# Linear attention with a routed feed-forward layer: accumulators of seven slots, token selection on ScalarE, and a bound order on GpSimd

## The chip, the cores and the metric

The kernel runs on one core of a Trainium2 chip. Its engines work beside one another, each through its own instructions in order: TensorE (PE in the profile; its weight loads are shown as PEld), VectorE (DVE), ScalarE (ACT), GpSimd (POOL) and SyncE (SP), which here only issues DMAs. The metric is the device time of one execution in microseconds (us), as the median of several runs.

## What is computed

A linear attention over 8 batches, 8 heads, 576 positions and head size 64, and behind it a layer of 8 experts in which each of the 4608 tokens goes to the one expert with the largest logit.

```python
def phi(x):
    proj = np.einsum('bhsd,df->bhsf', x, w_phi)                 # 64 -> 128
    proj = proj - np.max(np.abs(proj), axis=-1, keepdims=True)
    return np.concatenate([np.exp(proj), np.exp(-proj)], axis=-1)
q_p, k_p = phi(q), phi(k)
kv = np.einsum('bhsf,bhsd->bhfd', k_p, v)
z = np.sum(k_p, axis=2)
num = np.einsum('bhsf,bhfd->bhsd', q_p, kv)
den = np.einsum('bhsf,bhf->bhs', q_p, z)[..., None] + 1e-06
x = (num / den)                                                 # as rows: 4608 x 512
...
logits = x @ w_gate
expert_idx = np.argmax(logits, axis=1)
probs = softmax(logits)
h = np.maximum(xe @ w1[e], 0.0)                                 # xe: the rows of expert e
out[mask] = gate_w[mask, None] * (h @ w2[e])
```

## The kernel before

**Units and chunks.** The attention is worked in 16 units: four groups of two batches each (`NG`), and in each group four pairs of heads (`NPR`). The tokens of a group, 2 x 576, are nine chunks of 128 rows: chunks 0 to 3 are of the first batch, 4 to 7 of the second, and chunk 8, the tail, holds the last 64 rows of both. A unit goes through these stages:

- `load` and `split` bring k and q of the unit in two parts (three in unit 0) and write each as a rounded high part xh (on ACT) and a rest xl (mostly on POOL), since PE's products are made of three products of high and low parts.
- `project` multiplies by w_phi on PE (ps_proj) and subtracts the largest magnitude on DVE (tile t). `k_features` takes the two exponentials on ACT (tile e), `k_parts` splits them into kh (ACT) and kl: on POOL for chunk pairs 4 and 6, and from unit 1 on for pair 0, else on DVE. `q_features` transposes t on PE (pt) and takes the exponentials on ACT (qp).
- `v_parts` loads v and splits it into vh (ACT) and vl (POOL).
- `kv_steps` sums k's features against v on PE (pk, 30 products for each batch), `kv_copy` copies the sum on ACT (kvT), `fold_steps` multiplies it on PE with the tile fold (pf), which holds an identity and the gate's weights, so that one product later yields the numerator (64 columns), the denominator (1) and the gate's logits (8): 73 columns, `W`. DVE copies the result to kf.
- `num_steps` multiplies qp with kf on PE, into accumulators pn of six slots of 73 columns, with two buffers; a slot is a chunk of one of the two heads. There are four accumulators a unit: chunks 0 to 2, 3 to 5, 6 and 7, and the tail. Behind the last product of each, `normalize` or `normalize_tail` adds 1e-6 to the denominators, takes the reciprocal, and multiplies numerators (into xrow) and logits (into lgc), on DVE. After the tail, `store_rows` writes the unit's 128 columns of x to DRAM.

**What is done when.** Each unit has two halves. In the first, PE makes the sums over k and v of the previous unit's second batch, its fold, and the numerators of its chunks 0 to 3; in the second, the sums of its own first batch, and the previous unit's second fold and chunks 4 to 8. `half` writes the order of these products by hand and `ordered` binds it; the projections of the unit at hand and the next one are woven in by `merge`. What else runs when is set by a planner at build time: it goes through the program with assumed durations, gives each engine the earliest instruction in program order that is ready then, and so writes one fixed order for each engine, which the chip then follows with waits on semaphores. It moves work that is ready early far ahead: `constants2`, written in unit 2, runs at 13 us. `behind(m, other)` binds m behind other in the planner's order and adds no wait.

**Routing.** When a group's four units are done, `route` finds each token's expert, its rank in the expert and its gate: logits (a sum over lgc), largest logit, one-hot rows, counts, ranks, and then `select` for each of the nine chunks: two one-hot matrices of 128 x 128, with row number + 1 (sel_p) and the chunk's base (sel_h) in place of the one, from which PE later makes the list of tokens in each block. For groups 0 to 2 (`final is None`) the steps are spread over the units of the next group, one after every six products of a half (`spread`): the ranks and selections 0 to 6 fall into the second half of its second unit, selections 7 and 8 and the gate into the first half of its third. sel_p is made on DVE and sel_h on POOL. For the last group, routed in two parts, chunks 0, 2, 4, 6 and 8 are selected on ACT by `select_a`: y = |rank - column|, then relu(part1 - part1 * y), which is part1 where y is 0 and 0 elsewhere.

**Feed-forward.** After the attention, from 420 us on, blocks of 128 tokens are gathered by an indirect DMA, multiplied with the weights of their expert (split into wh on ACT and wl on DVE or POOL) and scattered to the output. `first_items` with the string `ORDER` writes the order of unit 0; there `C` stands for `constants`, which fills fold: a memset and eight copies on POOL, and a DMA of the gate's weights in ACT's queue.

Lines that come up: xl is L244, kl L284, kh L282, vl L312, kvT L353, pf L362, pn L386 (chunks) and L395 (tail), normalization L423 to L432 (tail L443 to L453), sel_p and sel_h L788, the ACT selection L780 to L782.

Of the kernel before, what the change touches and what calls it, by code (L numbers as in the profile page):

```python
# [9 lines left out]
F32 = mybir.dt.float32  # L10
# [3 lines left out]
AF = mybir.ActivationFunctionType  # L14
ALU = mybir.AluOpType
AX = mybir.AxisListType
# [3 lines left out]
P = 128  # L20
B, H, S, D = 8, 8, 576, 64
F = 128
DM = H * D
E = 8
# [3 lines left out]
NPR = H // 2  # L28
NC = 9
# [6 lines left out]
NU_ALWAYS = NU - 2  # L36

NSLOT = 7
NEARLY = (NG - 1) * NC
KD = DM // P  # L40
KF = FF // P
W = 73
# [7 lines left out]
def tile_linear_attention_moe(  # L50
# [12 lines left out]
    V, A, G, T = nc.vector, nc.scalar, nc.gpsimd, nc.tensor  # L63
# [21 lines left out]
    sm = late.enter_context(tc.tile_pool(name="sm", bufs=2, side="right"))  # L85
    sg = late.enter_context(tc.tile_pool(name="sg", bufs=1, side="right"))
    ps_kv = late.enter_context(tc.tile_pool(name="ps_kv", bufs=2, space=PSUM, side="right"))
    hold = mid.enter_context(tc.tile_pool(name="hold", bufs=1, side="right"))
    ps_nm = mid.enter_context(tc.tile_pool(name="ps_nm", bufs=2, space=PSUM, side="right"))
# [21 lines left out]
    fold = const.tile([D + 1, H, W], F32, name="fold")  # L111
# [8 lines left out]
    iota_p = const.tile([P, P], F32, name="iota_p")  # L120
# [4 lines left out]
    part1 = const.tile([P, 1], F32, name="part1")  # L125
    hb_i = const.tile([P, NG, NC], I32, name="hb_i")
    hbase = const.tile([P, NTILE], F32, name="hbase")
    neg1 = const.tile([P, 1], F32, name="neg1")
    neg_h = const.tile([P, NTILE], F32, name="neg_h")

    def constants():

        G.memset(fold, 0.0)
        for h in range(H):
            G.tensor_copy(fold[:, h, 0 : D + 1], ident[0 : D + 1, 0 : D + 1])
        nc.scalar.dma_start(fold[0:D, :, D + 1 : W], w_gate.rearrange("(h d) e -> d h e", d=D))
# [28 lines left out]
    sel_p = rt.tile([P, NTILE, P], BF16, name="sel_p")  # L165
    sel_h = rt.tile([P, NTILE, P], BF16, name="sel_h")
# [70 lines left out]
    def split(st, x, part, eh, el):  # L237

        n = st["ranges"][part][1] - st["ranges"][part][0]
        xr = st["raw", x, part]  # L240
        xh = inp.tile([P, CUT], F32R, name="xh", bufs=3)
        xl = inp.tile([P, CUT], F32R, name="xl", bufs=3)
        (A.copy if eh is A else eh.tensor_copy)(xh[:, 0:n], xr[:, 0:n])  # L243
        el.tensor_tensor(xl[:, 0:n], xr[:, 0:n], xh[:, 0:n], op=ALU.subtract)  # L244
        st["parts", x, part] = (xh, xl)

    def project(st, x, c0, n):
# [30 lines left out]
    def k_parts(st, c0, n):  # L278
        e, m = st["e", c0], 2 * n
        kh = kvp.tile([P, m, 2, F], F32R, name="kh", tag=f"kh{n}", bufs=3 * n - 1)  # L280
        kl = kvp.tile([P, m, 2, F], F32R, name="kl", tag=f"kl{n}", bufs=3 * n - 1)
        A.copy(kh, e[:, 0:m])  # L282
        eng = G if c0 in (4, 6) or (c0 == 0 and st["u"] > 0) else V
        eng.tensor_tensor(kl, e[:, 0:m], kh, op=ALU.subtract)  # L284
        for i in range(n):
            st["kp", c0 + i] = (kh, kl, 2 * i)

# [19 lines left out]
    def v_parts(st, u):  # L307
        vt = kvp.tile([P, NC * 2 + 2, D], F32, name="vt", bufs=1)
        nc.sync.dma_start(vt, vv[u])
        vh, vl = v_tiles[u % 2]  # L310
        A.copy(vh[:, :, 0:D], vt)
        G.tensor_tensor(vl, vt, vh[:, :, 0:D], op=ALU.subtract)  # L312
        st["v"] = (vh, vl)

    def v_load0(st, c0, c1):
# [62 lines left out]
    def num_steps(st, chunks):  # L378


        def step(c, hh, s):
            if c in (0, 3, 6, 8) and hh == 0 and s == 0:
                st["pn"] = ps_nm.tile([P, 6, W], F32, name="pn")
            qp, s0 = st["qp", c]
            if c < 8:
                m = T.matmul(  # L386
                    st["pn"][:, 2 * (c % 3) + hh, :],
                    qp[:, s, s0 + hh, :],
                    st["kf"][:, c // 4, hh, s, :],
                    start=(s == 0),  # L390
                    stop=(s == 1),
                )
            else:

                m = T.matmul(  # L395
                    st["pn"][:, 2 * hh : 2 * hh + 2, :],
                    qp[:, s, hh].rearrange("p b q -> p (b q)"),
                    st["kf"][:, :, hh, s, :],
                    start=(s == 0),
                    stop=(s == 1),  # L400
                )
            if c in (2, 5, 7, 8) and hh == 1 and s == 1:
                if c < 8:
                    normalize(st, c - c % 3, c % 3 + 1, st["pr"])
                else:
                    normalize_tail(st, st["pr"])
                    eng = G if st["g"] == NG - 1 and st["pr"] == 2 else nc.sync
                    store_rows(st["g"], st["x"], st["pr"] * P, P, eng=eng)
            return m

        return [
            (186 if c < 8 else 260, lambda a=(c, hh, s): step(*a))
            for c in chunks
            for hh in range(2)
            for s in range(2)
        ]

    def normalize(st, c0, n, pr):
        pn = st["pn"][:, 0 : 2 * n]
        if c0 == 0:  # L420
            st["x"] = hold.tile([P, NC, P], F32, name="xrow", bufs=2)
        rec = sm.tile([P, 6], F32, name="rec", bufs=2)[:, 0 : 2 * n]
        V.tensor_scalar_add(rec, pn[:, :, D], 1e-6)  # L423
        V.reciprocal(rec, rec)
        rb = rec.rearrange("p (c h) -> p c h", h=2).unsqueeze(3)
        V.tensor_tensor(
            st["x"][:, c0 : c0 + n, :].rearrange("p c (h d) -> p c h d", h=2),
            pn[:, :, 0:D].rearrange("p (c h) d -> p c h d", h=2),
            rb.to_broadcast([P, n, 2, D]),
            op=ALU.mult,  # L430
        )
        V.tensor_tensor(  # L432
            st["lgc"][:, c0 : c0 + n, 2 * pr : 2 * pr + 2, :],
            pn[:, :, D + 1 : W].rearrange("p (c h) e -> p c h e", h=2),
            rb.to_broadcast([P, n, 2, E]),
            op=ALU.mult,
        )

    def normalize_tail(st, pr):

        pn = st["pn"][:, 0:4].rearrange("p (h b) w -> p h b w", b=2)
        rec = sm.tile([P, 6], F32, name="rec", bufs=2)[:, 0:4].rearrange("p (h b) -> p h b", b=2)
        V.tensor_scalar_add(rec, pn[:, :, :, D], 1e-6)  # L443
        V.reciprocal(rec, rec)
        for b in range(2):
            rows = slice(D * b, D * b + D)
            V.tensor_tensor(
                st["x"][rows, 8, :].rearrange("p (h d) -> p h d", h=2),
                pn[rows, :, b, 0:D],
                rec[rows, :, b].unsqueeze(2).to_broadcast([D, 2, D]),  # L450
                op=ALU.mult,
            )
            V.tensor_tensor(  # L453
                st["lgc"][rows, 8, 2 * pr : 2 * pr + 2, :],
                pn[rows, :, b, D + 1 : W],
                rec[rows, :, b].unsqueeze(2).to_broadcast([D, 2, E]),
                op=ALU.mult,
            )

    def zipped(a, b):  # L460

# [13 lines left out]
    def behind(m, other):  # L475

        tc.add_manual_dep(
            m.ins,
            other.ins.name,
            mybir.DependencyInfo(mybir.DependencyClass.NoSync, mybir.DependencyReason.DATA),  # L480
            reason="order of the engine",
        )
# [164 lines left out]
    def route(g, lgc, c0, n, final=None):  # L647

        j0 = g * NC + c0
        js = slice(j0, j0 + n)  # L650
        r = {}
# [9 lines left out]
        def logits():  # L661
            V.tensor_reduce(
                tile_of("lg", [P, NC, E]),
                lgc[:, c0 : c0 + n].rearrange("p c h e -> p c e h"),
                axis=AX.X,
                op=ALU.add,
            )

# [115 lines left out]
        def select(c):  # L784
            if final is not None and c0 + c in ON_ACT:
                return select_a(c)
            for eng, dst, by in ((V, sel_p, part1), (G, sel_h, hbase[:, j0 + c : j0 + c + 1])):
                eng.tensor_scalar(  # L788
                    dst[:, j0 + c, :], iota_pb, r["rkr"][:, c : c + 1], by, op0=ALU.is_equal, op1=ALU.mult
                )  # L790
# [120 lines left out]
    for i in range(2):  # L911
        vh = kvp.tile([P, NC * 2 + 2, D + 2], F32R, name=f"vh{i}")
# [2 lines left out]
    deferred, prev = [], None  # L915
    units = []
    for g in range(NG):
        lgc = sm.tile([P, NC, H, E], F32, name="lgc")
        units += [{"u": g * NPR + pr, "g": g, "pr": pr, "lgc": lgc} for pr in range(NPR)]
    feats = feature_items(units[0], 0)  # L920
    for u, st in enumerate(units):
# [100 lines left out]
    st = {}  # L1022
# [19 lines left out]
    def weights(u, k):  # L1042
# [5 lines left out]
        w = max(0, u - 1)  # L1048
        slot = f"{k}_{w % 2}" if k < KD else f"s{(w * (NPC - KD) + k - KD) % NSLOT}"
        pool = wp0 if slot == "s0" or (k < KD and w % 2 == 0) else wp1 if slot in ("s1", "s2", "s3") else wpr  # L1050
# [153 lines left out]
    op = ctx.enter_context(tc.tile_pool(name="op", bufs=2, side="left", reuse_waits="tile"))  # L1204
# [151 lines left out]
```

## Time and profile before

| what | value |
|---|---|
| median of 3 runs | 924.06 us (922.11 to 924.46) |
| profiled execution | 923.96 us, span 922.3 us |
| mean granted clock of PE | 0.983 |
| PE busy, 50 to 75 us (a stretch of attention) | 24.81 of 25 us, clock 1.00 |
| PE busy, 0 to 25 us | 18.18 of 25 us, clock 0.93 |
| PE busy, 600 to 700 us (feed-forward) | 100.00 of 100 us, clock 1.00 |
| DVE, ACT, POOL busy over the span | 596.7, 590.5, 485.0 us |
| sel_p on DVE | 31 instructions, 18.8 us |
| normalization, multiplications of numerators | 32 of 128x384 at 551 ns, 16 of 128x256 at 421 ns, 32 of 64x128 at 286 ns |

How such lines are read: a group's row gives line, engine, operation, output and inputs with their shapes, the count, then busy time in us, the mean of one in ns, and the idle time of the engine just before them with what ended it. A timeline's row gives start and duration in us, engine, line, operation and tiles, how many were merged, and in brackets the idle time before it and what released it. A window's row gives its length, the busy time of PE, PEld, DVE, ACT and POOL with their instruction counts, PE's granted clock, the DMA share and GB/s. Idle time of an engine that nothing waits for costs nothing.

### The profile page before, as it was taken

Reading aid. Unit: us, or ns where it says so; the run is one execution under the profiler, and the core shown is the slowest. Engines: PE = TensorE matmul, PEld = TensorE weight load, DVE = VectorE, ACT = ScalarE, POOL = GpSimd, SP = SyncE. Lnnn points to the kernel's source line nnn. Section 1 sums busy time; section 2 is a strip of 40 time slices with the busy share of each in tenths; the row PEclk is TensorE's granted clock in tenths of the full one; section 3 lists DMA queues with packets and bytes.
Section 4 is the critical chain, followed back from the end, with each engine's and each line's share of the span. In section 5 each row is a group of like instructions: output and inputs, shape, how many; then the busy total and the mean of one; then the engine's idle time right before and its main releaser. Section 6 shows DMA issues by size and latency. Waiting matters only on the chain. (4 is left out here: it accounts for less than half of the span.)

```text
span 922.3 us, 18298 instructions
## 1 busy us (share of the span) xinstructions
PE 889.5 (96%) x6703; PEld 831.0 (90%) x6703; DVE 596.7 (65%) x1134; ACT 590.5 (64%) x900; POOL 485.0 (53%) x332
## 2 busy tenths in 40 slices
PE   7799999999999999999999999999999999999995
PEld 6799999999999999999799999999999999987883
DVE  7477788777987788759774444444444444457850
ACT  7577787777868776755565555555555555568951
POOL 7556668866676669734443333333333333337641
PEclk9799999999999999999999999999999999999998
DMA  5233433233334333243143143431434634764100
GB/s 154 80 96 107 107 106 103 68 100 102 93 93 108 106 107 93 76 129 108 59 154 122 45 152 115 155 112 44 153 114 158 215 113 149 229 206 129 46 24 15
DMA packets 64620, 102.44 MB, mean 111 GB/s; under 512 B 10702, under 2 KB 28622, under 8 KB 64528
## 3 DMA queue, kind: packets, MB, share of 16 engines
q1 hardware_dynamic: 57136, 80.31, 28.5%
q0 software_dynamic: 6720, 20.80, 7.3%
q8 instruction: 53, 0.87, 0.4%
q14 instruction: 39, 0.32, 0.1%
q10 hardware_dynamic: 672, 0.15, 0.1%
HBM read 136.81 MB, written 20.26 MB: 170 GB/s over the span
## 5 line engine op out<-in xcount | busy, mean ns | idle before, releaser
L1054 DVE TENSOR_TENSOR wl<-raw,wh 128x1024 fp32r<-128x1024 f32 x138 | 184.6, 1350 | 136.2 <-ACT wh L1053 136.1
L1053 ACT CAST wh<-raw 128x1024 fp32r<-128x1024 f32 x184 | 191.4, 1050 | 93.7 <-PE po L1120 66.2
L1054 POOL TENSOR_TENSOR wl<-raw,wh 128x1024 fp32r<-128x1024 f32 x46 | 113.3, 2469 | 175.0 <-ACT wh L1053 167.6
L386 PE MATMUL pn<-kf,qp 128*128 128x73 f32 x1024 | 156.8, 252 | 0.0
L1099 PE MATMUL pm<-xl,wh 128*128 128x256 f32 x544 | 154.1, 283 | 0.0
L1100 PE MATMUL pm<-xh,wl 128*128 128x256 f32 x544 | 154.1, 283 | 0.0
L1098 PE MATMUL pm<-xh,wh 128*128 128x256 f32 x544 | 153.4, 283 | 0.0
L386 PEld LDWEIGHTS pn<-kf,qp 128*128 128x128 f32 x1024 | 151.3, 190 | 0.1
L284 POOL TENSOR_TENSOR kl<-e,kh 128x1024 fp32r<-128x1024 f32 x47 | 112.4, 2392 | 50.7 <-ACT kh L282 47.9
L261 DVE TENSOR_REDUCE mx<-ps_proj 128x4 f32<-128x512 f32 (+1 forms) x160 | 101.2, 633 | 43.8 <-PE ps_proj L257 43.1
L244 POOL TENSOR_TENSOR xl<-xr,xh 128x512 fp32r<-128x512 f32 (+2 forms) x63 | 88.0, 1403 | 69.6 <-ACT xh L243 69.5
L1118 PE MATMUL po<-wh,hh 128*128 128x512 f32 x272 | 108.9, 401 | 0.0
L1119 PE MATMUL po<-wl,hh 128*128 128x512 f32 x272 | 106.8, 392 | 1.1 <-DVE wl L1054 1.1
L1099 PEld LDWEIGHTS pm<-xl,wh 128*128 128x128 f32 x544 | 104.1, 191 | 2.8 <-DVE xl L1081 0.4
L1098 PEld LDWEIGHTS pm<-xh,wh 128*128 128x128 f32 x544 | 104.0, 191 | 2.5
L1120 PE MATMUL po<-wh,hl 128*128 128x512 f32 x272 | 106.1, 390 | 0.0
L336 PE MATMUL pk<-kl,vh 128*65 128x256 f32 x320 | 99.8, 312 | 4.9 <-POOL kl L284 4.1
L1100 PEld LDWEIGHTS pm<-xh,wl 128*128 128x128 f32 x544 | 104.1, 191 | 0.2 <-issue 0.2
L262 DVE TENSOR_TENSOR t<-ps_proj,mx 128x512 f32<-128x512 f32 (+1 forms) x160 | 99.9, 632 | 3.2
L336 PE MATMUL pk<-kh,vh 128*65 128x256 f32 x320 | 100.6, 314 | 0.0
L336 PE MATMUL pk<-kh,vl 128*64 128x256 f32 x320 | 100.4, 314 | 0.0
L255 PE MATMUL ps_proj<-w_hi,xh 128*128 128x256 f32 x288 | 90.2, 313 | 4.2 <-DVE t L262 2.4
(232 smaller groups left out, 2010.9 us busy)
## 6 DMA issues: line engine op xcount, KB each, us to landing
raw<-w SPq DMA_DIRECT2D x184, 512.0 KB
vt<-vv SPq DMA_DIRECT2D x15, 640.0 KB
x_dram<-xrow SPq DMA_DIRECT2D x30, 256.0 KB
xr<-kT SPq DMA_DIRECT2D x15, 320.0 KB
xr<-qT SPq DMA_DIRECT2D x15, 320.0 KB
xr<-kT SPq DMA_DIRECT2D x17, 256.0 KB
xr<-qT SPq DMA_DIRECT2D x17, 256.0 KB
x_dram<-xrow SPq DMA_DIRECT2D x32, 32.0 KB
```

The source lines that it names most:

```text
L261: V.tensor_reduce(mx[:, 0 : 2 * n], psv, axis=AX.X, op=ALU.max, apply_absolute_value=True)
L284: eng.tensor_tensor(kl, e[:, 0:m], kh, op=ALU.subtract)
L336: return T.matmul(st["pk", bb][0:n, hh, :], (vl if j == 1 else vh)[:, 2 * (c + (bb if c == 8 else 0)) + hh, 0:n], (kl if j == 2 else kh)[: ...
L386: m = T.matmul(st["pn"][:, 2 * (c % 3) + hh, :], qp[:, s, s0 + hh, :], st["kf"][:, c // 4, hh, s, :], start=(s == 0), stop=(s == 1),)
L1053: A.copy(th, raw[k])
L1054: m = (G if k in (POOL_LO if u else POOL_LO0) else V).tensor_tensor(tl, raw[k], th, op=ALU.subtract)
L1098: T.matmul(pm[:, i], th, xh[:, k, :], start=(k == 0), stop=False)
L1099: T.matmul(pm[:, i], th, xl[:, k, :], start=False, stop=False)
L1100: T.matmul(pm[:, i], tl, xh[:, k, :], start=False, stop=(k == KD - 1))
L1118: T.matmul(po, hh[:, i, r], th[:, c], start=(i == j == 0), stop=False)
L1119: T.matmul(po, hh[:, i, r], tl[:, c], start=False, stop=False)
L1120: T.matmul(po, hl[:, i, r], th[:, c], start=False, stop=(i == 1 and j == 3))
```

## The change

Four things are edited.

1. pn gets seven slots (`SLOTS`), numbered through the unit by i = 2c + hh: slots 0 to 6, then 7 to 13, then 14 and 15 together with the tail's four. `normalize` serves all three and `normalize_tail` goes. The logits tile lgc changes its layout to one row of 18 slots per pair of heads, and the sum in `route` runs over two axes in place of one.
2. In `select`, groups 0 to 2 make sel_p by two ACT instructions, as `select_a` does, in place of one on DVE; sel_h stays on POOL.
3. `behind` binds, on POOL: the memset of fold behind the xl of unit 0's third part of k; unit 1's first xl of k behind unit 0's kl of chunk pair 4; and unit 1's vl behind its own kl of pair 0. For that, `split` and `k_parts` record their instructions.
4. The multiplications write x and lgc in slot order (`divide`).

```diff
+SLOTS = 7
...
-        G.memset(fold, 0.0)
+        behind(G.memset(fold, 0.0), units[0]["xl", "k", 2])
...
-        el.tensor_tensor(xl[:, 0:n], xr[:, 0:n], xh[:, 0:n], op=ALU.subtract)
+        m = el.tensor_tensor(xl[:, 0:n], xr[:, 0:n], xh[:, 0:n], op=ALU.subtract)
+        st["xl", x, part] = m
+        if (st["u"], x, part) == (1, "k", 0):
+            behind(m, units[0]["kl", 4])
...
-        eng.tensor_tensor(kl, e[:, 0:m], kh, op=ALU.subtract)
+        st["kl", c0] = eng.tensor_tensor(kl, e[:, 0:m], kh, op=ALU.subtract)
...
-        G.tensor_tensor(vl, vt, vh[:, :, 0:D], op=ALU.subtract)
+        m = G.tensor_tensor(vl, vt, vh[:, :, 0:D], op=ALU.subtract)
+        if u == 1:
+            behind(m, st["kl", 0])
...
-            if c in (0, 3, 6, 8) and hh == 0 and s == 0:
-                st["pn"] = ps_nm.tile([P, 6, W], F32, name="pn")
+            i = 2 * c + hh
+            if i % SLOTS == 0 and c < 8 and s == 0:
+                st["pn"] = ps_nm.tile([P, SLOTS, W], F32, name="pn")
...
-                    st["pn"][:, 2 * (c % 3) + hh, :],
+                    st["pn"][:, i % SLOTS, :],
...
-                    st["pn"][:, 2 * hh : 2 * hh + 2, :],
+                    st["pn"][:, 2 + 2 * hh : 4 + 2 * hh, :],
...
-            if c in (2, 5, 7, 8) and hh == 1 and s == 1:
-                if c < 8:
-                    normalize(st, c - c % 3, c % 3 + 1, st["pr"])
-                else:
-                    normalize_tail(st, st["pr"])
+            if s == 1 and (i % SLOTS == SLOTS - 1 or i == 17):
+                normalize(st, i - i % SLOTS, st["pr"])
+                if c == 8:
...
+        last = i0 == 2 * SLOTS
+        m = 6 if last else SLOTS
+        n = 2 if last else SLOTS
+        rec = sm.tile([P, SLOTS], F32, name="rec", bufs=2)
+        V.tensor_scalar_add(rec[:, 0:m], pn[:, 0:m, D], 1e-6)
+        V.reciprocal(rec[:, 0:m], rec[:, 0:m])
+        x = st["x"].rearrange("p c (h d) -> p (c h) d", h=2)
+        lg = st["lgc"][:, pr]
+
+        def divide(rows, dst, slots):
+            k = dst.stop - dst.start
+            r = rec[rows, slots].unsqueeze(2)
+            for t, c0, c1 in ((x, 0, D), (lg, D + 1, W)):
+                V.tensor_tensor(
+                    t[rows, dst], pn[rows, slots, c0:c1], r.to_broadcast([rows.stop - rows.start, k, c1 - c0]), op=ALU.mult
+                )
+
+        divide(slice(0, P), slice(i0, i0 + n), slice(0, n))
+        if last:
+            for b in range(2):
+                divide(slice(D * b, D * b + D), slice(16, 18), slice(2 + b, 6, 2))
...
-                lgc[:, c0 : c0 + n].rearrange("p c h e -> p c e h"),
-                axis=AX.X,
+                lgc[:, :, 2 * c0 : 2 * c0 + 2 * n].rearrange("p r (c h) e -> p c e r h", h=2),
+                axis=AX.XY,
...
-            for eng, dst, by in ((V, sel_p, part1), (G, sel_h, hbase[:, j0 + c : j0 + c + 1])):
+            by = hbase[:, j0 + c : j0 + c + 1]
+            if final is None:
+                y = sg.tile([P, P], F32, name="y", bufs=2)
+                A.activation(y, iota_p, AF.Abs, bias=r["rkr"][:, c : c + 1], scale=-1.0)
+                A.activation(sel_p[:, j0 + c, :], y, AF.Relu, bias=part1, scale=neg1)
+            for eng, dst, by in ((G, sel_h, by),) if final is None else ((V, sel_p, part1), (G, sel_h, by)):
...
-        lgc = sm.tile([P, NC, H, E], F32, name="lgc")
+        lgc = sm.tile([P, NPR, 2 * NC, E], F32, name="lgc")
```

More of the change, by code (lines that the diff above doesn't have):

```diff
@@ L416, in num_steps, with normalize @@
         ]
-    def normalize(st, c0, n, pr):
-        pn = st["pn"][:, 0 : 2 * n]
-        if c0 == 0:
+    def normalize(st, i0, pr):
+        pn = st["pn"]
+        if i0 == 0:
             st["x"] = hold.tile([P, NC, P], F32, name="xrow", bufs=2)
[L422 to L458, printed above, removed]
+        last = i0 == 2 * SLOTS
```

## The prediction

> **What bounds the kernel now.** I read the page first, then who waits for whom on TensorE (PE), then windows around each wait, then the timelines of the engines there.
>
> ```profile
> span 922.3 us, 18298 instructions
> PE 889.5 (96%) x6703; PEld 831.0 (90%) x6703; DVE 596.7 (65%) x1134; ACT 590.5 (64%) x900; POOL 485.0 (53%) x332
> ```
>
> PE is busy for 889.5 of 922.3 us, and the change adds and removes no matrix product. So all that can be won is PE's 32.8 us of idle time, and the time in which PE runs at a lower granted clock. The waits of PE, in us in total, times, longest:
>
> ```profile
> PE pn L395 <- DVE lgc L432: 5.8, 3, 1.9
> PE pk L336 <- POOL kl L284: 4.1, 1, 4.1
> ...
> PE ps_proj L255 <- ACT xh L243: 1.8, 1, 1.8
> ...
> PE pf L362 <- ACT kvT L353: 0.9, 5, 0.2
> ...
> PE pn L395 <- DVE rec L424: 0.8, 1, 0.8
> ```
>
> The first two are what the change aims at: three waits of 1.9 us, one in the routing of each early group, and one of 4.1 us near the start. The windows show what a wait costs besides (length, then busy time of PE, PEld, DVE, ACT, POOL; clock; DMA share; GB/s):
>
> ```profile
> 25.00:50.00 25.00, 20.95 (x146) 20.35 (x147) 13.18 (x23) 16.40 (x31) 11.92 (x7) 0.80 0.23 72
> ...
> 150.00:160.00 10.00, 8.06 (x63) 7.86 (x62) 9.00 (x26) 4.80 (x11) 10.00 (x9) 0.84 0.61 181
> ...
> 350.00:360.00 10.00, 8.09 (x59) 7.90 (x59) 8.50 (x25) 3.93 (x8) 10.00 (x9) 0.83 0.64 186
> 151.30:173.90 22.60, 20.55 (x173) 20.10 (x171) 19.94 (x52) 13.66 (x27) 19.06 (x16) 0.92 0.41 109
> ```
>
> In each of the three stages (first and last shown) PE idles 1.9 us of ten, and the clock falls to 0.84 of full, which is another 1.6 us of work. I take 3.5 us as the loss of a stage, 10.5 us for three. At the start, 25 to 50 us, it is 4.05 us idle and a fifth of 25 us, 5 us, in clock. The Trainium skill's "TensorE: Matmul & The Clock Gate" (HAM oscillation) has it that the clock drops after an idle gap of over about 3.4 us; by it three gaps of 1.9 us would cost only themselves, 5.8 us. The row of 0.84 behind a wait of 1.9 us says otherwise, and the row decides.
>
> **What makes the wait in the routing stages.** One stage, on DVE, POOL and PE (start, duration; in brackets the idle time before):
>
> ```profile
> 151.53 3.52 DVE L788 TENSOR_SCALAR sel_p<-iota_pb,rkr,part 128x128 bf16<-128x128 bf16 x2
> ```
> ```profile
> 151.08 2.69 POOL L312 TENSOR_TENSOR vl<-vt,vh 128x1280 fp32r<-128x1280 f32 x1
> 153.74 1.25 POOL L244 TENSOR_TENSOR xl<-xr,xh 128x512 fp32r<-128x512 f32 x1
> ```
> ```profile
> 156.20 0.49 PE L395 MATMUL pn<-kf,qz 128*128 128x146 f32 x2 [1.94 <-DVE lgc L432]
> ```
>
> Two selections take 3.52 us and end when POOL's two subtractions do (153.74 + 1.25 = 154.99): they stood still behind POOL. The normalization of c 3 to 5 is queued behind them on DVE; the tail's products (c = 8) open the fourth accumulator, take the buffer of those chunks, and so wait.
>
> **Part 1: three accumulators of 7.** The third accumulator now holds c 7 and the tail and takes the buffer of slots 0 to 6, normalized half a unit earlier. The wait on lgc goes by this alone, even if DVE stood still again, and so does the single 0.8 us on rec at the end of attention. What DVE saves:
>
> ```profile
> L424 DVE RECIPROCAL rec<-rec 128x6 f32<-128x6 f32 x32 | 6.0, 186 | 0.5
> ```
> ```profile
> L423 DVE TENSOR_SCALAR rec<-pn 128x6 f32<-128x6 f32 x32 | 5.2, 161 | 14.8 <-PE pn L386 14.4
> ```
>
> Multiplications stay 10 a unit over the same elements; one add and one reciprocal go, 18 instructions become 16: 0.35 us a unit, 5.6 us in 16 units, on an engine at 65%: nothing by itself. Logits read as many elements as before: nothing, at most some tenths in the last group, where the first route must now wait for chunk 6. I take a gain of 0.5 us at the tail, between 1 lost and 1.5 won.
>
> **Part 2: 27 selections to ScalarE (ACT).** What goes and what comes:
>
> ```profile
> L788 DVE TENSOR_SCALAR sel_p<-iota_pb,rkr,part 128x128 bf16<-128x128 bf16 x31 | 18.8, 640 | 0.0
> ```
> ```profile
> L781 ACT ACTIVATE sel_p<-y,part,neg 128x128 bf16<-128x128 f32 x5 | 2.4, 483 | 0.0
> ...
> L780 ACT ACTIVATE y<-iota_p,rkr 128x128 f32<-128x128 f32 x5 | 1.8, 392 | 0.1
> ```
> ```profile
> 429.90 0.70 ACT L780 ACTIVATE y<-iota_p,rkr 128x128 f32<-128x128 f32 x2
> 430.50 0.48 ACT L781 ACTIVATE sel_p<-y,part,neg 128x128 bf16<-128x128 f32 x1
> 430.89 0.48 ACT L782 ACTIVATE sel_h<-y,hbase,neg_h 128x128 bf16<-128x128 f32 x1
> ```
>
> DVE loses 27 x 0.64 = 17 us, and nothing on ACT stands still behind POOL. The final groups run the same two operations already, without a table load between them. In a row they start 0.30 us (two y in 0.60) and 0.39 us apart: 0.69 us a selection, 6.2 us a stage; laid end to end they are 0.875 us, 7.9 us. I take 0.69, since y has two buffers. Where do 6.2 us lie?
>
> ```profile
> 153.38 0.20 ACT L711 CAST base_b<-base 128x8 bf16<-128x8 f32 x1
> 158.72 0.58 ACT L353 COPY kvT<-pk 65x512 f32<-65x512 f32 x1 [5.13 <-PE pk L336]
> ```
> ```profile
> 160.50 0.34 PE L362 MATMUL pf<-fold,kvT 65*128 65x73 f32 x2
> ...
> 164.50 0.32 PE L336 MATMUL pk<-kl,vh 128*65 128x256 f32 x1
> ```
> ```profile
> 158.99 2.38 POOL L284 TENSOR_TENSOR kl<-e,kh 128x1024 fp32r<-128x1024 f32 x1
> ```
>
> From the ranks' end (151.3) to the second fold behind them (173.9) ACT is busy 13.66 of 22.6 us. With 6.2 more it needs 19.8, so ACT alone lets a stage get shorter by 2.8 us at most, not by 3.5. POOL's kl for chunk 6 ends at 161.37; the product that needs it, at 164.50, would come 3.5 us earlier, at 161.0: POOL caps the gain at 3.1. The narrow place is the kvT copy. ACT comes free at 153.58 and idles 5.13 us; without PE's wait kvT's products end near 155.2 (158.72 less 3.5) and the fold wants the copy at 157.0 (160.50 less 3.5). ACT runs in order. Selections 0 to 6 stand ahead of the copy in program order; if four of them are ahead of it, it ends at 153.58 + 4 x 0.69 + 0.58 = 156.9, in time; if all seven are, at 159.0, 2.0 us late. Between these I take 1.0 us late. In half of the cases the clock will fall again, half of 1.6. PE can pull some projections forward over that gap, but the next half waits for exp and casts that ACT now makes later: I set these against each other, save for one more wait of 0.2 us on the next kvT (longest of the row above). A stage gains 3.5 - 1.0 - 0.8 - 0.2 = **1.5 us**, three 4.5 us, bounds -9.6 (the slower rival) and 8.4 (ACT's cap).
>
> **Part 3: POOL's order in the first units.**
>
> ```profile
> 20.05 2.72 POOL L312 TENSOR_TENSOR vl<-vt,vh 128x1280 fp32r<-128x1280 f32 x1
> 22.72 1.54 POOL L244 TENSOR_TENSOR xl<-xr,xh 128x640 fp32r<-128x640 f32 x1
> 24.21 2.34 POOL L284 TENSOR_TENSOR kl<-e,kh 128x1024 fp32r<-128x1024 f32 x1
> ```
> ```profile
> 20.39 1.04 ACT L282 CAST kh<-e 128x1024 fp32r<-128x1024 f32 x1
> ...
> 27.73 0.60 ACT L302 ACTIVATE qp<-pt 128x512 f32<-128x512 f32 x1 [4.29 <-PE pt L293]
> ```
> ```profile
> 26.61 0.34 PE L336 MATMUL pk<-kl,vh 128*65 128x256 f32 x1 [4.08 <-POOL kl L284]
> ...
> 32.99 0.39 PE L255 MATMUL ps_proj<-w_hi,xh 128*128 128x256 f32 x1 [1.79 <-ACT xh L243]
> ```
>
> Unit 1's vl and xl go behind kl of unit 0's chunk 4. Its kh ends at 21.43, so kl runs 21.4 to 23.8 and PE waits 1.3 us, not 4.08: 2.75 us won there. More would come of the clock (0.80 in this window), but the next wait, 32.99, is on ACT, which idled 4.29 us for PE and then works almost without a pause to that xh: that end moves by ACT's 2.75 us and not by PE's pace. What is queued behind: xl waits for kl, until 25.4, before unit 1's first product; vl waits for kl of unit 1's chunk 0:
>
> ```profile
> 44.04 2.40 POOL L284 TENSOR_TENSOR kl<-e,kh 128x1024 fp32r<-128x1024 f32 x1
> ```
> ```profile
> 49.91 0.28 PE L336 MATMUL pk<-kh,vl 128*64 128x256 f32 x1
> ```
>
> 46.4 + 2.7 = 49.1, 0.8 us before PE wants it: covered, barely. The memset of fold goes from idle POOL time behind xl of k part 2, near 10 us; its eight copies follow, and the gate's DMA, which waits for the memset in ACT's queue, with them:
>
> ```profile
> 1.56 0.69 ACTq L136 DMA_DIRECT2D fold<-w_gate  x1
> ```
>
> That is 0 to 0.7 us on an ACT with small pauses; I take 0.25. Part 3 gains 2.75 - 0.25 = **2.5 us**, bounds 0 (a wait of the same kind on vl) and 4.5 (the clock holds as well).
>
> **Sum.** 2.5 + 4.5 + 0.5 = 7.5 us, off the profiled execution's 923.96 us (span 922.3 and 1.7 around it; the median of the three runs, 924.06, is 0.1 more): **916.5 us**.
>
> **Rivals.** *ACT hides it all.* The planner puts the selections into ACT's pauses and kvT ahead of them: 2.8 a stage, 4.5 at the start, 0.8 at the tail, 13.7: 910.3 us. For it: 5.13 us of ACT idle right there. Against: nearly all of that idle time is PE's wait itself. Chance 0.18. *ACT gives it back.* The wait on lgc becomes a wait of the same size on kvT, and the start alone remains: 923.96 - 2.5 = 921.5 us. For it: ACT's 0.2 us waits on kvT show no slack half a unit later. Chance 0.22. *Slower: kvT behind all selections.* All nine, laid end to end, run ahead of the copy: it ends at 153.58 + 7.9 + 0.58 = 162.1, 5.1 us after the fold wants it (157.0), and the clock falls (1.6): 6.7 us lost where 3.5 were won, 3.2 a stage, 9.6 us, less 2.5 at the start: 931.1 us. It decides once more than 3.5 - 1.6 = 1.9 us of lateness stand at the fold: from seven selections ahead at 0.69 each. Chance 0.17, the planner's new order at the start included. The Trainium skill's "ScalarE: Activation LUTs" (Rules for kernel authors) speaks for these two: it wants relu-like work on VectorE, not ScalarE. The row of 3.52 us is why I do not follow it. *No effect at all* would need the waits to be elsewhere; the rows name them, so it gets no chance of its own.
>
> **How the numbers follow.** The forecast (912.5 to 919.5) has 0.43, the rivals 0.18, 0.22 and 0.17. Range: down to 908.5, below the first rival, and up to 927.0, which leaves out some 0.04 below and most of the slower rival. About 0.3%, 2.8 us, is what a measurement of this kernel can tell from no change: faster means below 921.2, slower above 926.7. Faster: 0.43 + 0.18 + 0.07 of the second rival = 0.68; same 0.15; slower 0.17.
>
> **What would show it.** Right: no wait of pn on lgc; DVE without an instruction of 3 us between 150 and 156; PE's wait at kl near 1.3 us; ACT busy some 20 of 21 us from the ranks to the second fold; clock above 0.84 there. Wrong: waits of pf on kvT of 1 us and more in three places (ACT is the bound), a wait of pk on vl near 47 us (the bound order is too tight), or a new wait at the tail's logits.

## The result: 0.8% slower, and the profile after

| | before | after |
|---|---|---|
| median of 15 runs | 923.33 us (922.00 to 927.24) | 932.27 us (927.15 to 934.84) |
| ratio, 95% interval | 1 | 1.0083 (1.0065 to 1.0101) |
| profiled execution, span | 923.96, 922.3 us | 933.36, 931.6 us |
| mean granted clock of PE | 0.983 | 0.979 |

The forecast was 916.5 us and its range ended at 927.0: sign and range were wrong. The page of after begins like this:

```profile
span 931.6 us, 18305 instructions
...
PE 892.9 (96%) x6703; PEld 831.5 (89%) x6703; DVE 588.1 (63%) x1075; ACT 607.9 (65%) x954; POOL 479.3 (51%) x332
```

PE runs the same 6703 products, and its idle time grew from 32.8 to 38.7 us (931.6 - 892.9). ACT is 17.4 us more busy, as the change says. DVE is only 8.6 us less busy, where the forecast took away 17 for the selections and 5.6 for the normalization: its 16 kl of 128x512 now take 1.37 us on average in place of 0.73, 10.2 us in all, as they now run beside two-input operations of POOL (one is shown below). Who waits for whom on PE, in us in total, times, longest:

```profile
PE ps_proj L261 <- POOL xl L245: 7.7, 6, 2.1
...
PE pk L342 <- POOL kl L288: 2.5, 4, 0.8
PE pt L297 <- ACT y L780: 2.1, 3, 0.7
...
PE pm L1093 <- DVE hl L1101: 1.7, 1, 1.7
```

The wait of pn on lgc (5.8 us) and those on kl and xh at the start (4.1 and 1.8 us) are gone. In their place PE waits for xl on POOL, for kl there, for ACT at a y of the selection (y is no input of that product; which earlier work of ACT it needs there, the profile doesn't say), and in the tail for hl, which DVE makes for the feed-forward.

**Where the time went.** ACT copies kvT twice a unit, 32 times in all, each time behind the same products, so its start is a milestone. In ACT's timelines of before and of after (start, duration), copies 10 and 14 bracket the first routing stage and copy 32 ends the attention's sums (before's copy 10 was at 145.60 us, its copy 32 at 412.73):

```profile
196.56 0.57 ACT L353 COPY kvT<-pk 65x512 f32<-65x512 f32 x1
```
```profile
136.35 0.58 ACT L359 COPY kvT<-pk 65x512 f32<-65x512 f32 x1
...
194.15 0.58 ACT L359 COPY kvT<-pk 65x512 f32<-65x512 f32 x1
...
419.56 0.58 ACT L359 COPY kvT<-pk 65x512 f32<-65x512 f32 x1 [5.46 <-PE pk L342]
```

After is 9.25 us ahead when the first stage begins and 2.4 us ahead behind it: the stage takes 57.80 us in place of 50.96. The table cuts the span of each profile at copies 10, 14, 18, 22, 26 and 30 (the three routing stages are 10 to 14, 18 to 22, 26 to 30) and gives the difference to before in us. Beside it stand PE's idle time in the three stages, in us, and the number of PE's products in them. The kernels e1 to e9 are told below; each row is one profiled execution.

| kernel | start | three stages | between and behind them | after copy 32 | span | PE idle in the stages | products in the stages |
|---|---|---|---|---|---|---|---|
| before | | | | | | 6.0 | 1376 |
| after | -9.3 | +6.8 +5.8 +6.3 = +18.9 | -2.8 | +2.5 | +9.3 | 13.5 | 1422 |
| e1 order only | -7.7 | -2.4 | 0.0 | 0.0 | -10.0 | 6.3 | 1376 |
| e2 selection only | +0.3 | -3.2 | 0.0 | +0.2 | -2.8 | 6.7 | 1376 |
| e3 seven slots only | -1.9 | +14.4 | -1.8 | +2.1 | +12.8 | 13.5 | 1411 |
| e4 seven slots and order | -10.7 | +12.0 | -1.8 | +1.1 | +0.6 | 11.9 | 1411 |
| e5 as e4, sel_h bound | -9.7 | +1.2 | -1.8 | +3.7 | -6.6 | 5.5 | 1411 |
| e6 after, sel_h bound | -10.6 | +11.3 | -2.8 | +1.9 | -0.2 | 10.5 | 1422 |
| e7 order and selection | -8.9 | 0.0 | +0.1 | 0.0 | -8.8 | 6.7 | 1376 |
| e8 as e1, nine sel_h first | -8.7 | +2.4 | 0.0 | +0.1 | -6.2 | 8.1 | 1376 |
| e9 as e5, six slots in the last unit | -11.1 | +1.1 | -1.8 | -0.5 | -12.3 | 5.6 | 1411 |

So the start won far more than the 2.5 us forecast, and three stages that should have won 4.5 us are 18.9 us longer. The lengths are not all loss, though. The first stage of before and of after, as windows (length, busy time of PE, PEld, DVE, ACT, POOL with their counts, clock, DMA share, GB/s):

```profile
145.60:196.56 50.96, 48.90 (x440) 48.39 (x439) 41.54 (x102) 37.43 (x67) 38.48 (x26) 0.97 0.36 92
```
```profile
136.35:194.15 57.80, 53.33 (x456) 51.89 (x456) 40.84 (x94) 45.33 (x89) 38.91 (x27) 0.94 0.33 86
```

With seven slots, projections and transposes that before made ahead of copy 10 or between the stages fall into the stages. Such a product took 0.09 to 0.16 us of PE (14 fewer of them shorten PE's work between the first two stages by 1.25 us from e1 to e5; 12 more lengthen that of the first stage by 2.0 us, the clock 1.00 each time). By that, an estimate, 4 to 8 of after's 18.9 us are moved work, and 3 to 6 us in e3, e4, e5 and e9. PE's idle time leaves that out: it grew by 7.4 us in after's stages. The rest fits the clock, 0.94, 0.97 and 0.94 in place of 0.97 in each.

One of the stages in after, on POOL, on PE, on ACT and on DVE (start, duration, in brackets the idle time before):

```profile
146.35 7.00 POOL L783 TENSOR_SCALAR sel_h<-iota_pb,rkr,hbase 128x128 bf16<-128x128 bf16 x9
153.32 2.35 POOL L288 TENSOR_TENSOR kl<-e,kh 128x1024 fp32r<-128x1024 f32 x1
...
160.26 2.37 POOL L288 TENSOR_TENSOR kl<-e,kh 128x1024 fp32r<-128x1024 f32 x1 [2.36 <-ACT kh L286]
162.59 2.50 POOL L245 TENSOR_TENSOR xl<-xr,xh 128x512 fp32r<-128x512 f32 x2
```
```profile
155.73 0.33 PE L342 MATMUL pk<-kl,vh 128*65 128x256 f32 x1 [0.80 <-POOL kl L288]
...
163.91 0.39 PE L261 MATMUL ps_proj<-w_hi,xl 128*128 128x256 f32 x1 [2.08 <-POOL xl L245]
165.14 0.58 PE L261 MATMUL ps_proj<-w_hi,xl 128*128 128x256 f32 x1 [0.49 <-POOL xl L245]
```
```profile
150.54 0.58 ACT L359 COPY kvT<-pk 65x512 f32<-65x512 f32 x1
...
157.35 0.87 ACT L781 ACTIVATE sel_p<-y,part,neg 128x128 bf16<-128x128 f32 x2
...
160.01 1.14 ACT L244 CAST xh<-xr 128x512 fp32r<-128x512 f32 x2
```
```profile
153.72 2.50 DVE L288 TENSOR_TENSOR kl<-e,kh 128x512 fp32r<-128x512 f32 x1
```

Before, POOL made five sel_h, then kl of pair 6 (at 158.99 us), then four:

```profile
154.99 4.04 POOL L788 TENSOR_SCALAR sel_h<-iota_pb,rkr,hbase 128x128 bf16<-128x128 bf16 x5
...
161.37 3.62 POOL L788 TENSOR_SCALAR sel_h<-iota_pb,rkr,hbase 128x128 bf16<-128x128 bf16 x4
```

Now all nine run ahead of kl. And ACT makes the two xh of the next unit only behind the last selections; POOL's xl follows them, behind one more kl, and PE waits 2.08 and 0.49 us for xl. The window shows the clock behind that, 0.73, where the lowest window of before's stage has 0.84:

```profile
160.00:170.00 10.00, 7.43 (x43) 6.80 (x42) 3.79 (x6) 5.85 (x12) 4.83 (x3) 0.73 0.23 62
```

kvT is not late: PE's list of waits has no entry for it in after, where before had five. Two theories follow. *Order*: seven slots change the planner's order on POOL, and the nine sel_h ahead of kl cost the time. *ACT*: the selections cost it, by xh. They need not exclude each other.

### The profile page after: what moved, and what is told of

Same layout as the page of the kernel before. It is cut to its first block, busy times and chain, and to the rows that moved or that the text cites. A ratio compares the mean times of both kernels' runs of the same rounds, so it can differ in the third digit from the quotient of the medians.

```text
span 931.6 us, 18305 instructions
## 1 busy us (share of the span) xinstructions
PE 892.9 (96%) x6703; PEld 831.5 (89%) x6703; DVE 588.1 (63%) x1075; ACT 607.9 (65%) x954; POOL 479.3 (51%) x332
## 5 line engine op out<-in xcount | busy, mean ns | idle before, releaser
L393 PE MATMUL pn<-kf,qp 128*128 128x73 f32 x1024 | 160.4, 255 | 2.8 <-DVE kf L379 2.7
L393 PEld LDWEIGHTS pn<-kf,qp 128*128 128x128 f32 x1024 | 153.8, 193 | 4.7 <-DVE kf L379 4.6
```

Of the source, the lines that this page charges most:

```text
L393: m = T.matmul(st["pn"][:, i % SLOTS, :], qp[:, s, s0 + hh, :], st["kf"][:, c // 4, hh, s, :], start=(s == 0), stop=(s == 1),)
```

## The experiments

Times are medians. Before was run again beside e1 to e4 (922.56 us), beside e5 to e8 (922.61) and beside e9 to e12 (924.06); ratios, with their 95% intervals, are against these.

**Each part alone: e1, e2, e3, and e4 without the selection.** e1 is before with the three bindings:

```diff
-        G.memset(fold, 0.0)
+        behind(G.memset(fold, 0.0), units[0]["xl", "k", 2])
...
+        if (st["u"], x, part) == (1, "k", 0):
+            behind(m, units[0]["kl", 4])
...
+        if u == 1:
+            behind(m, st["kl", 0])
```

> The kernel before with the three bound orders on GpSimd alone (six-slot accumulators, selections on VectorE). Theory A (the order gains the 8.5 us by which the changed kernel leads at its second kvT copy, and touches nothing in the routing stages): some 915 us, a ratio of 0.991, with the three waits of pn on lgc of 1.9 us still there. Theory B (the lead at the start comes from all edits together, through the planner): under 4 us gained, 920 us or more.

Measured: 914.05 us, ratio 0.9912 (0.9885 to 0.9939). That is as Theory A has it. In the profile 7.7 of its 10.0 us lie in the start. The waits on lgc are still there, three of them, in total 5.8 us; the 2.4 us in the stages are the clock, which was 1.00 in two of them in place of 0.97.

e2 is before with the selection of after:

```diff
...
+            if final is None:
+                y = sg.tile([P, P], F32, name="y", bufs=2)
+                A.activation(y, iota_p, AF.Abs, bias=r["rkr"][:, c : c + 1], scale=-1.0)
+                A.activation(sel_p[:, j0 + c, :], y, AF.Relu, bias=part1, scale=neg1)
+            for eng, dst, by in ((G, sel_h, by),) if final is None else ((V, sel_p, part1), (G, sel_h, by)):
...
```

> The kernel before with the early groups' sel_p on ScalarE alone. Theory A (selections on ScalarE push the casts xh of the next unit's parts back, GpSimd's xl comes late and PE waits for it, some 4.7 us a stage more than in the changed kernel's own surroundings): the waits of pn on lgc are gone, waits of projections on xl appear, and the kernel is slower by some 5 to 14 us, 929 to 938 us. Theory B (the routing stages lose by the seven-slot accumulators): the stages gain up to 2.8 us each, 915 to 922 us.

Measured: 922.31 us, 0.9993 (0.9973 to 1.0012): no change that the runs can tell, though the profile's stages are 3.2 us shorter in all. The lgc waits go and PE's waits for xl come, 5.2 us in four, as Theory A has it, but not A's loss of 5 to 14 us: PE idles 6.7 us in the stages, hardly more than before's 6.0, and the shorter stages are the clock (1.00 in all three).

e3 is before with the seven slots, e4 is e3 with the bindings, that is, after with sel_p on DVE:

```diff
-            for eng, dst, by in ((G, sel_h, by),) if final is None else ((V, sel_p, part1), (G, sel_h, by)):
+            for eng, dst, by in ((V, sel_p, part1), (G, sel_h, hbase[:, j0 + c : j0 + c + 1])):
```

> The kernel before with three accumulators of seven slots alone (selections on VectorE, GpSimd's order free). Theory A: the waits on lgc go by the accumulators alone, as the tail no longer takes a buffer that is late, and each stage gains most of its 3.5 us: 912 to 918 us. Theory B (the accumulators make the stages and the end of attention worse): 925 to 935 us.

> The changed kernel with the early groups' sel_p back on VectorE: accumulators and bound order together. Theory A: the start's 8.5 us stay, the routing stages no longer lose 4.7 us each; 905 to 915 us, faster than both. Theory B (accumulators to blame): the stages still lose, 927 us or more.

Measured: e3 936.96 us, 1.0148 (1.0115 to 1.0181); e4 926.61 us, 1.0046 (1.0030 to 1.0062). Theory A is refuted in both, and e3 loses even more than B's range. Seven slots alone cost 14.4 us against before, and 12.6 us on top of the bindings (926.61 - 914.05). POOL and PE in the first stage of e3, then PE in that of e4:

```profile
153.70 7.67 POOL L774 TENSOR_SCALAR sel_h<-iota_pb,rkr,hbase 128x128 bf16<-128x128 bf16 x9
161.34 1.26 POOL L245 TENSOR_TENSOR xl<-xr,xh 128x512 fp32r<-128x512 f32 x1
162.56 2.33 POOL L286 TENSOR_TENSOR kl<-e,kh 128x1024 fp32r<-128x1024 f32 x1
```
```profile
164.94 0.48 PE L338 MATMUL pk<-kl,vh 128*65 128x256 f32 x1 [3.77 <-POOL kl L286]
```
```profile
155.65 0.33 PE L342 MATMUL pk<-kl,vh 128*65 128x256 f32 x1 [3.06 <-POOL kl L288]
```

Nine sel_h and an xl stand ahead of kl on an engine without a pause, and PE waits. The selection on ACT has no part in it: it isn't in these kernels. The new layout of lgc and the one `normalize` come with the slots in every kernel and were not tried apart.

**Is it the order? e5 and e6.** Both bind sel_h of chunks 5 to 8 behind kl of pair 6, where before had them by itself; e5 is e4, e6 is after with this edit:

```diff
+                m = eng.tensor_scalar(
...
+                if final is None and eng is G and c >= 5:
+                    behind(m, units[NPR * (g + 1) + 1]["kl", 6])
```

> Seven-slot accumulators and the bound order, selections on VectorE, and GpSimd's sel_h of chunks 5 to 8 bound behind the kl of chunk pair 6, so that five stand ahead of it and four behind, as in the kernel before. Theory A (the accumulators lose because the planner then puts all nine sel_h ahead of that kl, and PE waits 3 us for it in each of three stages): the waits of pk on kl fall from 8.6 us to under 2, some 915 us. Theory B (the accumulators lose by themselves): it stays at 924 to 929 us.

> The changed kernel with the same binding of sel_h 5 to 8 behind the kl of pair 6. Theory A: kl comes 3 us earlier, xl behind it too, the waits of projections on xl (7.7 us) fall to about half; 918 to 924 us. Theory B: no gain beyond 2 us, 930 to 933 us.

Measured: e5 914.73 us, 0.9898 (0.9867 to 0.9929); e6 923.51 us, 0.9999 (0.9980 to 1.0019). With sel_p on DVE the binding gives back 11.9 us (926.61 - 914.73), nearly all that the seven slots cost: it was the order. PE's waits for POOL's kl fall from 8.6 to 0.8 us in all, as Theory A has it. POOL, DVE and PE in e5:

```profile
143.25 2.69 POOL L316 TENSOR_TENSOR vl<-vt,vh 128x1280 fp32r<-128x1280 f32 x1
145.93 3.99 POOL L778 TENSOR_SCALAR sel_h<-iota_pb,rkr,hbase 128x128 bf16<-128x128 bf16 x5
...
151.14 2.37 POOL L288 TENSOR_TENSOR kl<-e,kh 128x1024 fp32r<-128x1024 f32 x1
```
```profile
143.28 3.59 DVE L778 TENSOR_SCALAR sel_p<-iota_pb,rkr,part 128x128 bf16<-128x128 bf16 x4
```
```profile
155.67 0.36 PE L259 MATMUL ps_proj<-w_hi,xh 128*128 128x256 f32 x1 [0.89 <-DVE t L266]
```

The order is that of before again. DVE still stands still behind vl (four selections in 3.59 us, the first of them until vl ends; the next five, beside sel_h, take 0.30 to 0.37 each). PE no longer waits for lgc, but a wait for t has come, 0.89 us here. So even with the order mended PE idles 5.5 us in the three stages, against 6.3 in e1 and 6.0 in before, which keep the waits on lgc: most of that wait was not removed, it moved. In e6 the binding gives back 8.8 us (932.27 - 923.51). That leaves 8.8 us between e5 and e6, which differ in the selection alone. PE's waits for xl in e6:

```profile
PE ps_proj L261 <- POOL xl L245: 7.4, 7, 1.9
```

The time of e6 is what Theory A expects, but not in A's way: the waits for xl were to fall by half and are nearly as before the binding (7.7 us). What fell is PE's wait for kl, from 2.5 to 0.2 us, PE's idle time in the stages, from 13.5 to 10.5, and the loss by the clock (0.97 in each stage). Part of xh's lateness, too, came from POOL: in after ACT idles 2.47 us for POOL's kl just ahead of the last selections, in e6 it doesn't, and xh begins 23.7 us after copy 10 in after, 21.7 in e6. So both theories hold, each for a share. Why the planner turns the order with seven slots, the traces don't show.

**ACT's share with six slots: e7**, before with the bindings and the selection (the diffs of e1 and e2 together).

> Bound order and selections on ScalarE with the old six-slot accumulators. Theory A (the parts add up, and the loss is the accumulators' alone): 914.0 less up to 1.3, 912.5 to 914 us, the fastest so far. Theory B (the three edits only lose together, through ScalarE): 917 us or more.

Measured: 914.57 us, 0.9898 (0.9868 to 0.9928), e1's time. The selection removes the lgc waits and wins nothing, a little over Theory A's range and well under B's: PE idles 6.7 us in the stages, e1 6.3. That the stages are 2.4 us longer than e1's is the clock, 0.97 in two of them where e1 had 1.00; from before to e2 the same edit made them 3.2 us shorter. So with six slots the selection costs nothing that the runs can tell, and with seven and the order bound it costs 8.8 us (e6 against e5), 4.9 of them idle time of PE in the stages (10.47 - 5.54). A difference is in ACT's order; in the first stage of e7, on ACT and POOL:

```profile
141.96 0.62 ACT L243 CAST xh<-xr 128x512 fp32r<-128x512 f32 x1
```
```profile
144.87 1.28 POOL L244 TENSOR_TENSOR xl<-xr,xh 128x512 fp32r<-128x512 f32 x1
```

Here one of the two xh runs ahead of the selections, and its xl ahead of all sel_h. In after and e6 both stand behind. That this is the reason is argued from the order: no kernel binds that xh ahead of the selections with seven slots.

**The order, reversed: e8** puts it into the kernel without seven slots: e1 with all nine sel_h issued with the first selection.

```diff
+                if c == 0:
+                    for i in range(n):
+                        G.tensor_scalar(sel_h[:, j0 + i, :], iota_pb, r["rkr"][:, i : i + 1], ...)
```

> The bound order alone, six-slot accumulators, selections on VectorE and GpSimd, but all nine sel_h written ahead of the first sel_p, so that GpSimd runs nine in a row ahead of the kl of pair 6, as it does with the new accumulators. Theory A: PE waits some 2 to 4 us for that kl in each stage, and the kernel loses 6 to 15 us against 914.0: 920 to 929 us. Theory B (the place of sel_h does not matter): 913 to 916 us.

Measured: 917.91 us, 0.9948 (0.9922 to 0.9973): 3.9 us over e1, in the expected direction but less than expected, and its interval overlaps e1's a little. Its waits on PE:

```profile
PE pn L400 <- DVE lgc L437: 5.8, 3, 1.9
PE pk L341 <- POOL kl L287: 2.3, 3, 1.7
```

In the first stage e8 waits 0.4 us for kl, e4 3.06. The orders aren't quite the same: in e8 the xl stands ahead of the sel_h, not behind, so that kl begins 17.0 us after copy 10 and not 18.4 as in e4. Besides, PE has already lost 1.9 us on lgc in e8 when it comes to kl, and nothing in e4. That fits one wait covering the other, so that taking one away shows the other at its full size; it also means that this order with six slots, beside the lgc waits, explains 3.9 of the 12.6 us.

**The tail: e9** is e5 with the four old accumulators in the last unit only.

```diff
...
+            six = st["u"] == NG * NPR - 1
+            SLOTS = 6 if six else 7
+            if (i % SLOTS == 0 and c < 8 or six and i == 16) and s == 0:
...
```

> As with the accumulators, the bound order and sel_h bound behind kl (914.7), but the last unit keeps the old four accumulators. Theory A (the seven slots cost 1 to 3.7 us behind the last kvT copy, because the last group's first route, chunks 0 to 5, must wait for chunk 6): that time goes, the wait of pm on hl (1.7) too; 911 to 913.5 us. Theory B (the end loses for another reason, the clock or the order of weights): 914 to 916 us.

Measured: 912.56 us (911.75 to 913.88), 0.9876 (0.9847 to 0.9905). The cost behind copy 32 goes from +3.7 in e5 to -0.5. In e5, PE's wait for hl and the window there:

```profile
420.56 0.58 PE L1090 MATMUL pm<-xh,wh 128*128 128x256 f32 x1 [1.66 <-DVE hl L1098]
```
```profile
420.00:430.00 10.00, 9.44 (x52) 9.32 (x53) 8.14 (x35) 7.63 (x16) 1.78 (x4) 0.66 0.07 4
```

In e9 that wait is 0.96 us, not gone as Theory A had it, and the clock from 420 to 430 us is 1.00. The two profiles exaggerate: e5's is the slowest of its four runs (917.38 us), e9's the fastest (911.75). e4 has the wait of 1.66 us too, kept a clock of 1.00 in the 20 us behind copy 32, and lost 1.1 us there. e9 is the fastest kernel of the study and beats both before and after; its interval overlaps those of e1, e5 and e7, so the last 2 us are not settled.

**Which binding? e10, e11, e12** are before with one of the three each: the xl, the vl, the memset of fold.

> The kernel before with one of the three bindings: unit 1's first xl behind unit 0's kl of pair 4. In the plan vl still stands ahead of that kl. Theory A (each wait is what stood ahead on GpSimd): the wait at kl falls from 4.1 to some 2.5 us, since vl (2.7) ahead ends at 22.8; 920 to 922 us. Theory B (this binding brings the gain of the order): 914 us.

> The kernel before with one of the three bindings: unit 1's vl behind its own kl of pair 0. In the plan xl still stands ahead of unit 0's kl of pair 4. Theory A: the wait at kl falls from 4.1 to under 2 us; 917 to 921 us. Theory B: 914 us.

> The kernel before with one of the three bindings: the memset of fold behind xl of k's third part. GpSimd's plan of the first 40 instructions is then the same as with all three. Theory A (this one binding moves the planner to the whole new order): 914 us, as with all three. Theory B (the memset itself has no weight, and the other two make the gain): 921 to 924 us.

Measured: e10 921.71 us, 0.9985 (0.9961 to 1.0010); e11 921.61 us, 0.9971 (0.9952 to 0.9990); e12 915.82 us, 0.9922 (0.9890 to 0.9955). e10 is as its Theory A, e11 just above A's range, and e12 close to A's 914: the memset's binding alone does what all three do, as near as the runs can tell. PE's waits in e10, then POOL and ACT in e12:

```profile
PE pk L339 <- POOL kl L287: 2.8, 1, 2.8
...
PE ps_proj L258 <- ACT xh L243: 1.8, 1, 1.8
```
```profile
19.87 2.40 POOL L285 TENSOR_TENSOR kl<-e,kh 128x1024 fp32r<-128x1024 f32 x1
22.22 3.09 POOL L244 TENSOR_TENSOR xl<-xr,xh 128x640 fp32r<-128x640 f32 x2
```
```profile
21.60 0.73 ACT L243 CAST xh<-xr 128x640 fp32r<-128x640 f32 x1
```

With xl bound, vl still stands ahead of kl, and with vl bound, xl does: PE waits 2.8 and 2.2 us. With the memset bound, the planner by itself puts both behind kl, and on ACT it puts the second xh, which ran at 32.22 us before, at 21.60.

## Why the prediction was wrong, point by point

- **What bounds the kernel**: right as to the places. But the price of a wait in clock was taken as fixed, and as 0.16 of ten us, 1.6; PE was busy for only 8.06 of the ten, which makes 1.3. e1 keeps the three waits; the windows that hold its second and third:

```profile
240.00:250.00 10.00, 8.05 (x75) 7.87 (x74) 9.57 (x29) 5.36 (x11) 10.00 (x10) 1.00 0.59 171
...
340.00:350.00 10.00, 8.09 (x59) 7.89 (x58) 8.51 (x26) 3.99 (x8) 10.00 (x9) 0.83 0.63 186
```

  The same wait costs no clock in the one and a sixth in the other. e1's first two stages are 1.15 and 1.14 us shorter than before's, the third 0.09, with the same number of products: the clock was worth some 1.1 us, and only where it fell. The Trainium skill ("TensorE: Matmul & The Clock Gate", What's actually happening) says that the clock's window is free-running and that the point at which the clock changes depends on where in it the first product lands. These rows are in keeping with that. They do not fit its idle window of about 3.4 us, since a wait of 1.9 us was enough here. The forecast's 3.5 us a stage was too much even for the trace of before, 1.9 of wait and some 1.1 to 1.3 of clock.
- **Part 1**: right that the waits on lgc and on rec go by the slots alone. The step that failed is "nothing by itself". It counted DVE's instructions, which was right (48 adds and 48 reciprocals in place of 64 each), and took POOL's order as given. The planner's order changed, nine sel_h ran ahead of kl, and three stages grew by 14.4 us (e3), 7.5 of them idle time of PE, where the forecast had a gain; with the order bound PE idles there as little as before (e5). Part 2's own line, that POOL's kl caps the gain, named the place, but only as a cap.
- **Part 1, the tail**: +0.5 us was forecast, with 1 lost as the bound; with seven slots in every unit it lost 1.1 to 3.7 us in five profiles, the least in the one whose clock stayed at 1.00 there (e4). e9 points at the last unit's slots, but its time isn't clear of e5's. That the first route waits for chunk 6 was named and priced at some tenths; PE's wait for hl and the clock behind it were not.
- **Part 2**: right on the price of ACT's work (the 27 y have a median of 399 ns, the 27 sel_p of 490, where the quoted rows have means of 392 and 483) and that kvT stays in time. The step that failed is "I set these against each other, save for one more wait of 0.2 us": the casts that ACT now makes later are xh, and PE's waits for xl came to 7.7 us (0.7 in before), besides the clock. By the medians the selection costs 5.7 us with seven slots (932.27 against e4's 926.61) and 8.8 with seven and sel_h bound, where the forecast had 4.5 won with Part 1; with six it costs nothing that can be told (e7, e2). Why it costs so much more with seven is open, beyond the place of xh.
- **Part 3**: right that kl behind xl and vl makes the wait: kl begins at 21.32 us in after, forecast 21.4, and PE's wait for it is 0.20 us, forecast 1.3:

```profile
21.32 2.39 POOL L288 TENSOR_TENSOR kl<-e,kh 128x1024 fp32r<-128x1024 f32 x1
```
```profile
23.77 0.33 PE L342 MATMUL pk<-kl,vh 128*65 128x256 f32 x1 [0.20 <-POOL kl L288]
```

  Mis-sized: 2.5 us forecast, 7.7 measured to copy 10 with the bindings alone (e1), and more than the bound of 4.5. After's 9.3 have 15 fewer products ahead of copy 10. The step that failed is "that end moves by ACT's 2.75 us": ACT's xh moved forward too, its wait went, and the clock held:

```profile
25.00:50.00 25.00, 24.00 (x221) 23.61 (x220) 18.11 (x34) 23.16 (x41) 19.37 (x12) 1.00 0.32 97
```

  The clock in that window, seen at 5 us and left out of the sum, was half of the gain: up to copy 10 e1 runs before's 1127 products with 3.9 us less of idle time and 3.8 us less of busy time. And the binding costed at a loss of 0.25 us, the memset, carries the gain by itself (e12).
- **The rivals**: after lies near the slower rival's 931.1 us, but not by its mechanism: PE has no wait for kvT in after. Its first half, ACT's work late, was right for xh. Nothing had been given to the case that decided: that the planner's order on POOL turns. None of the three signs of being wrong that the prediction names (waits on kvT, on vl, on the tail's logits) is in after's list of waits.

## What to carry to other kernels

Where a planner writes the order, an edit is not priced by its own instructions: first compare the order of each engine before and after around the products that the path waits for, above all on an engine without pauses. More buffers can take away one wait and show the next at its full size; where slack work (here sel_h) and needed work (kl, xh) share an engine, bind the slack work behind the needed. A binding that looks like tidying can move the rest of the plan, so the parts of such a change are to be measured apart.

## What the runs showed of the hardware

- DVE's selections stood still behind POOL's vl, which has two inputs, but ran beside sel_h, which has one (e5: 3.59 us for four, then 0.30 to 0.37 each). DVE's kl of 128x512, with two f32 inputs, took 2.50 us beside POOL's kl in after, against a mean of 0.73 in before. Whether the second input or the type (f32 against bf16) decides wasn't tried.
- In the profiles, the granted clock of the first 25 us lay between 0.80 and 1.00, with no pattern that I can see: e1 and e12 run POOL's first operations in the same order, had 0.80 and 0.93, and their first kvT copies differ by 1.6 us (29.34 and 27.77). The column "start" is uncertain by as much.
- After's 15 runs spread over 7.7 us, before's over 5.2. Why is open.
